# One weight load written as eight strided loads: w_mod in an adaLN decode block

## The chip, the core and the metric

The kernel runs on one core of a Trainium2 chip. A core has five engines with queues of their own: TensorE (PE; its weight loads are listed as PEld), VectorE (DVE), ScalarE (ACT), GpSimd (POOL) and SyncE (SP), which here only issues transfers. Sixteen DMA engines move data between HBM and SBUF, the on-chip memory of 128 partitions. The metric is the device time of one execution in microseconds (us), given as the median of several runs.

## What is computed

One decode step (a batch of two, one token each) of a block with adaptive layer norm: attention over the last 1024 positions of a cached sequence, then a gated feed-forward part. D is 640, there are 32 heads of 192, F is 1536, and everything in HBM is bf16. Cut to what matters:

```python
mod = (silu(c) @ w_mod).reshape(2, 6, 1, 640)     # w_mod: 640 x 3840
sa, ca, ga, sb, cb, gb = mod[:, 0], ..., mod[:, 5]
h = layernorm(x) * (1 + ca) + sa
x = x + ga * attention(h)      # q = h @ wq; K and V: the last 1024 positions of the caches; then @ wo
h = layernorm(x) * (1 + cb) + sb
x = x + gb * ((gelu(h @ w_gate) * (h @ w_up)) @ w_down)
```

## The kernel before

The program first builds a list of operations for each engine and then emits each list in order. An operation names the buffers that it reads and writes; from these names a small scheduler (class `_Sched`, lines 28 to 101) works out which semaphore values it has to wait for. A transfer (`S.dma`) adds 16 to its semaphore when it has landed; `k_dma` (line 239) makes the transfer itself, so that every transfer is listed under line 240. Waits are put ahead of the waiting operation on its own engine's queue (`emit`, line 93), so that everything behind it in that queue waits too.

Loads. Nearly all of them are issued by SP in one fixed order:

1. `ld_wm` (line 294): w_mod, 4,915,200 bytes. Row p of the 128 partitions takes rows 5p to 5p+4 of w_mod, which is 38,400 contiguous bytes of HBM. It lands in the tile r3.
2. `ld_wq` (line 295): the query weights, 128 rows of 61,440 bytes, into the tile r1.
3. The cache loads (line 321), in the order k0, k1, k2, v0, k3, v1 and so on. For each pair of heads and each of K and V there is one slot of a ring of six (`NS`), filled by two transfers, one per batch entry. Each of the two goes to every second partition: 64 rows of 12,288 bytes. The first six slots have no wait. A later one waits until the slot's earlier contents have been used: by the score matmuls (`p_reduce`, line 443) for K, or by `p_pv` (line 488) for V.
4. The output weights wo in four transfers (line 561), the feed-forward weights (lines 565 to 573), with waits on the parts of r1 and r3 that they overwrite.

Four small loads of c and x, four rows of 320 bytes each, are issued by ACT (lines 248 to 251).

Compute ahead of attention. Silu of c (line 332) and a transpose give `scT`. `mod_part(0)` (lines 367 to 385) multiplies it with the first half of w_mod in 20 matmuls, which need all 128 partitions of w_mod, and ACT copies the result to `modC`. `layer_norm("ln1")` follows, then `mod_part(1)`, and two copies (line 389) that lay the normalised row out as the matmul weights `hbm`. The query units (`q_unit`, line 396) multiply `hbm` with slices of wq; the first cannot start before wq has landed.

Attention. A software pipeline over the 16 pairs of heads (lines 526 to 556) multiplies each K slot in place with the query on DVE (`d_mul`, line 431), sums over the head dimension with identity matmuls on PE (`p_reduce`), takes a softmax, and multiplies with the V slot (`p_pv`). PE also runs filler matmuls (line 420).

After attention come the wo matmuls (line 576), the second layer norm, gate and up (`ffn_gu`, line 592), the down projection (line 610), and two small stores of the result (line 625).

Of the kernel before, what the change touches and what calls it, by code (L numbers as in the profile page):

```python
# [103 lines left out]
def bass_adaLN_cond__sliding_block_cached__geglu_ffn__decode_kernel(  # L104
# [15 lines left out]
    P = 128  # L120
    B, _, D = A_x.shape
# [11 lines left out]
    KT = D // P  # L133
# [15 lines left out]
    BIG = -1.0e30  # L149

    NS = 6
    NWO = 4
    GPC = NGG // NWO
    WD_SPLIT = [6, 4, 2]
# [6 lines left out]
    with es:  # L161
        S = _Sched(nc, es)
# [6 lines left out]
        r3 = sb("r3", [P, R3N], BF16)  # L169
# [5 lines left out]
        qbc = sb("qbc", [P, NG, Dh], BF16)  # L175
        ring = sb("ring", [P, NS, J, Dh], BF16)
        ident_b = sb("ident_b", [P, P], BF16)
# [13 lines left out]
        scT = sb("scT", [P, KT, SQ], BF16)  # L191
# [33 lines left out]
        def bank(k):  # L225
            return ("bank", k)
# [3 lines left out]
        sem_wm = S.sem("d_wm")  # L230
        sem_wq = S.sem("d_wq")
        sem_wo = [S.sem("d_wo%d" % i) for i in range(NWO)]
        sem_wg = S.sem("d_wg")
        sem_wu = S.sem("d_wu")
        sem_wd = [S.sem("d_wd%d" % i) for i in range(len(WD_SPLIT))]
        sem_ring = [S.sem("d_ring%d" % i) for i in range(NS)]
        sem_out = [S.sem("d_out%d" % i) for i in range(2)]

        def k_dma(dst, src):
            return lambda e: e.dma_start(dst, src)  # L240
# [9 lines left out]
        for b in range(2):  # L250
# [5 lines left out]
             reads=["ones_f"], writes=["ident_f"], name="ident_f")  # L256
        S.op("pool", lambda e: e.tensor_copy(out=ident_b[:, :], in_=ident_f[:, :]),
             reads=["ident_f"], writes=["ident_b"], name="ident_b")
# [5 lines left out]
             reads=["ones_f"], writes=["par8"], name="par8")  # L264
        S.op("pool", lambda e: e.affine_select(out=noff[:, :], in_=zero_f[:, :], pattern=[[-1, HB]],
                                               compare_op=ALU.is_equal, fill=BIG, base=0, channel_multiplier=1),
             reads=["zero_f"], writes=["noff"], name="noff")
        S.op("pool", lambda e: e.memset(SEL[:, :, :, :], 0.0), writes=["SEL"], name="SEL0")
        S.op("pool", lambda e: e.memset(DS[:, :, :], 1.0), writes=["DS"], name="DS1")
        hb0 = S.op("pool", lambda e: e.memset(hbm_v, 0.0), writes=["hbm"], name="hbm0")  # L270
        S.op("dve", lambda e: e.memset(ps[:, BK_O, 0:ON], 0.0), writes=[bank(BK_O)], name="init_O")
        S.op("dve", lambda e: e.tensor_reduce(out=G32[:, :], in_=ident_f[:, :].rearrange("p (a m) -> p m a", m=SQ), axis=AX.X, op=ALU.add),
             reads=["ident_f"], writes=["G32"], name="G32")
        S.op("dve", lambda e: e.tensor_reduce(out=P4[:, :], in_=ident_f[:, :].rearrange("p (q c) -> p c q", c=HB), axis=AX.X, op=ALU.add),
             reads=["ident_f"], writes=["P4"], name="P4")
        S.op("dve", lambda e: e.tensor_copy(out=Bsel[:, :].rearrange("p (a m) -> p a m", m=SQ),
                                            in_=G32[:, :].unsqueeze(1).broadcast_to([P, NJ, SQ])),
             reads=["G32"], writes=["Bsel"], name="Bsel")

        for z in range(2):  # L280
            for jj in range(2):
# [3 lines left out]
                    reads=["G32"], writes=["SEL"], name="SEL%d%d" % (z, jj))  # L285
            S.op("dve", (lambda z: lambda e: e.memset(DS[:, z, :].rearrange("p (a m) -> p a m", m=SQ)[:, :, 0:2], 0.0))(z),
                 writes=["DS"], name="DS0%d" % z)
# [3 lines left out]
                reads=["P4"], writes=["DS"], name="DS%d" % z)  # L291

        keep = {}
        keep["wm_dma"] = S.dma("sp", k_dma(r3[:, 0:KT * 6 * D], w_mod.rearrange("(p k) n -> p (k n)", k=KT)), sem_wm, writes=["wm"], name="ld_wm")
        keep["wq_dma"] = S.dma("sp", k_dma(r1[:, :], A_wq.rearrange("(p k) n -> p (k n)", k=KT)), sem_wq, writes=["wq"], name="ld_wq")


# [9 lines left out]
        def slot_of(kind, g):  # L307
            return place[(kind, g)] % NS

# [3 lines left out]
        def declare_ring(*consumed):  # L313
            ring_state["done"].update(place[it] for it in consumed)
            while ring_state["next"] < len(items) and (ring_state["next"] < NS or (ring_state["next"] - NS) in ring_state["done"]):
                s = ring_state["next"]
                kind, g = items[s]
                slot = s % NS
                cache = A_v_cache if kind == "v" else A_k_cache
# [45 lines left out]
        mod_pe = []  # L365

        def mod_part(part):
            bk = MB[part]

            def f(e):  # L370
                last = None
                for k in range(KT):
                    for j in range(NJ):
                        last = e.matmul(ps[SQ * j:SQ * j + SQ, bk, 0:3 * DN].rearrange("p (i n) -> p i n", i=3), lhsT=scT[:, k, :],  # L374
                                        rhs=wm_v[:, k, 3 * part * D:3 * (part + 1) * D].rearrange("p (i n) -> p i n", i=3)[:, :, DN * j:DN * j + DN],
                                        start=(k == 0), stop=(k == KT - 1), tile_position=(0, SQ * j))
                return last
            mod_pe.append(S.op("pe", f, reads=["scT", "wm"], writes=[bank(bk)], name="mod%d" % part))
            S.op("act", lambda e: e.activation(out=modC[:, 3 * part:3 * part + 3, :].rearrange("p i n -> p (i n)"),
                                               in_=ps[:, bk, 0:3 * DN], func=ACTF.Copy),  # L380
                 reads=[bank(bk)], writes=[("modC", part)], name="mod%d_evac" % part)
            S.op("dve", lambda e: e.tensor_scalar(out=opc[:, part, :], in0=modC[:, 3 * part + 1, :], scalar1=1.0, scalar2=None, op0=ALU.add),
                 reads=[("modC", part)], writes=[("opc", part)], name="opc%d" % part)

        mod_part(0)
        layer_norm("ln1", 0, 0)
        mod_part(1)
        for h in range(2):
            S.op("dve", (lambda h: lambda e: e.tensor_copy(
                out=hbm_v[:, :, h, :].rearrange("p k (q e b) -> p k q e b", e=2, b=2)[:, :, :, h, :],  # L390
                in_=hT[:, :, 0:2].unsqueeze(2).broadcast_to([P, KT, QP, 2])))(h),
                reads=["hT"], writes=["hbm"], name="hbm%d" % (h + 1))

        qst = {"n": 0, "last": None}
# [164 lines left out]
        r1_dead = [keep["wq_dma"], qst["last"]]  # L559
        for ci in range(NWO):  # L560
            S.dma("sp", k_dma(wo_v[:, ci * GPC * ST:(ci + 1) * GPC * ST, :].rearrange("p (g s) n -> p g (s n)", s=ST),
                              A_wo[ci * GPC * ST * P:(ci + 1) * GPC * ST * P, :].rearrange("(g p s) n -> p g (s n)", p=P, s=ST)),
                  sem_wo[ci], writes=[("wo", ci)], deps=r1_dead, name="ld_wo%d" % ci)
        r3_dead = [keep["wm_dma"], qst["last"], hb0] + mod_pe
        S.dma("sp", k_dma(wg_v.rearrange("p k n -> p (k n)"), B_w_gate.rearrange("(p k) n -> p (k n)", k=KT)), sem_wg,
              writes=["wg"], deps=r3_dead, name="ld_wg")
        S.dma("sp", k_dma(wu_v.rearrange("p k n -> p (k n)"), B_w_up.rearrange("(p k) n -> p (k n)", k=KT)), sem_wu,
              writes=["wu"], deps=r3_dead, name="ld_wu")
# [6 lines left out]

        for ci in range(NWO):
            def f(e, ci=ci):
                last = None
                for t in range(ci * GPC * ST, (ci + 1) * GPC * ST):
                    for j in range(NJ):  # L580
                        last = e.matmul(ps[SQ * j:SQ * j + SQ, BK_M, 0:DN], lhsT=oT[:, t, :], rhs=wo_v[:, t, DN * j:DN * j + DN],  # L581
                                        start=(t == 0), stop=(t == NT - 1), tile_position=(0, SQ * j), skip_group_check=True)
                return last
# [3 lines left out]
             reads=[bank(BK_M), ("modC", 0)], writes=[("lnt", 0)], name="ga_attn")  # L587
        S.op("dve", lambda e: e.tensor_tensor(out=X2[:, 0, :], in0=lnt[:, 0, :], in1=X2[:, 0, :], op=ALU.add),
             reads=[("lnt", 0)], writes=[("X2", 0)], name="x1")
        layer_norm("ln2", 1, 3)  # L590

        def ffn_gu(bk, wv, key):
            def f(e):
# [10 lines left out]
             reads=[bank(BK_Q[0])], writes=["gl"], name="gelu")  # L604
        ffn_gu(BK_Q[1], wu_v, "wu")
        S.op("dve", lambda e: e.tensor_tensor(out=aC[:, :], in0=ps[:, BK_Q[1], 0:FN], in1=gl[:, :], op=ALU.mult),
             reads=[bank(BK_Q[1]), "gl"], writes=["aC"], name="geglu")
        to_contraction(aT[:, :, :], aC[:, :], FT, ["aC"], ["aT"], "aT")
        f0 = 0
        for ci, nf in enumerate(WD_SPLIT):  # L610
            def f(e, f0=f0, nf=nf):
# [10 lines left out]
             reads=[bank(BK_C), ("modC", 1)], writes=["fin"], name="gb_y")  # L622
        S.op("dve", lambda e: e.tensor_tensor(out=orow[:, :], in0=fin[:, :], in1=X2[:, 0, :], op=ALU.add),
             reads=["fin", ("X2", 0)], writes=["orow"], name="outC")
# [55 lines left out]
```

## Time and profile before

| | |
|---|---|
| median of 3 runs | 190.42 us (190.39 to 190.46) |
| the profiled execution | 191.04 us |
| its span, first to last instruction | 189.3 us |
| mean granted TensorE clock | 0.902 |
| HBM read | 76.88 MB |
| PE, DVE, ACT busy | 69%, 48%, 16% of the span |
| w_mod, from issue to landing | 14.5 us |
| wq, from issue to landing | 32.2 us |

The profile is taken from one execution by the hardware profiler. The span leaves out what lies ahead of the first and behind the last instruction of the program, so the execution's own time is 1.74 us longer than its span. Its page has, among other things: busy time in 40 equal slices of the span (4.73 us each), with the share of time in which the sixteen DMA engines were busy and the rate that they moved; the chain of work that ended last; the costliest groups of instructions; and the issues of transfers with the time from issue to landing. The trace behind the page also holds a record of every packet that a DMA engine moved (queue, start, duration, bytes). A row of a transfer, contiguous at both ends, is one packet; each transfer ends on each of its engines with a packet of 4 bytes that writes its semaphore.

### The profile page before, as it was taken

The numbers are of one execution on the slowest core, as the hardware profiler recorded it, in microseconds if no ns is written. First come the engines' busy times: TensorE is split into PE (matmuls) and PEld (weight loads), VectorE is DVE, ScalarE is ACT, GpSimd is POOL, SyncE is SP. The second block draws the span as 40 slices with busy tenths as digits, with TensorE's granted clock in tenths as the row PEclk, the third lists the DMA queues.
The fourth block names the chain that finished last, engine by engine and source line by source line (L and its number), as shares of the span: only waits on it lengthen the run. The fifth ranks groups of instructions, "written<-read, shape, count | busy, mean of one in ns | idle before, by whom it ended". The sixth has DMA issues, their size and how long they took to land.

```text
span 189.3 us, 2631 instructions
## 1 busy us (share of the span) xinstructions
PE 131.5 (69%) x1100; PEld 65.8 (35%) x1100; DVE 91.5 (48%) x140; ACT 29.6 (16%) x75; POOL 3.8 (2%) x15
## 2 busy tenths in 40 slices
PE   0004500989999999997897797898987886333443
PEld 0001200445545435443443343334433454333212
DVE  7101600194855974954956857658559221003421
ACT  1002200122142210210210120120121224000310
POOL 8000000000000000000000000000000000000000
PEclk9999999999999999999999999999999955555555
DMA  7999997999999999999999999999999999999980
GB/s 252 398 507 454 454 415 319 428 418 435 431 415 434 416 430 418 431 419 428 421 436 421 423 423 428 421 421 428 426 428 416 426 417 422 414 433 435 403 328 3
DMA packets 7275, 77.04 MB, mean 407 GB/s; under 512 B 1248, under 2 KB 1248, under 8 KB 2656
## 3 DMA queue, kind: packets, MB, share of 16 engines
q1 hardware_dynamic: 7224, 76.88, 96.5%
q8 instruction: 8, 0.13, 0.3%
q14 instruction: 3, 0.02, 0.0%
q10 hardware_dynamic: 40, 0.01, 0.0%
HBM read 76.88 MB, written 0.00 MB: 406 GB/s over the span
## 4 chain that ended last, share of the span: by engine, by line
DMA 57%; PE 23%; SPq 9%; DVE 8%; issue 1%; ACT 0%; DVEq 0%
DMA ring<-in_A_k_cache_dram 23%; DMA r<-in_A_wq_dram 17%; DMA r<-in_B_w_up_dram 17%; PE ps L446 11%; SPq L240 9%; DVE ring L433 7%; PE ps L406 6%; PE ps L423 1%; PE ps L615 1%; PE ps L597 1%; PE ps L496 1%; PE ps L476 0%; DVE aT L330 0%; PE ps L463 0%; PE ps L477 0%
## 5 line engine op out<-in xcount | busy, mean ns | idle before, releaser
L433 DVE TENSOR_TENSOR ring<-ring,qbc 128x6144 bf16<-128x6144 bf16 x16 | 53.7, 3354 | 33.7 <-DMA ring<-in_A_k_cache_dram 19.9
L446 PE MATMUL ps<-ring,ident_b 128*128 128x512 bf16 x192 | 45.8, 380 | 9.3 <-DVE ring L433 9.3
L446 PEld LDWEIGHTS ps<-ring,ident_b 128*128 128x128 bf16 x192 | 17.9, 98 | 33.0 <-DVE ring L433 14.5
L423 PE MATMUL ps<-qbc,ident_b 128*128 128x512 bf16 x104 | 26.8, 380 | 0.0
L406 PE MATMUL ps<-r 128*128 128x384 bf16 x80 | 15.2, 347 | 11.5 <-DMA r<-in_A_wq_dram 11.5
L503 ACT ACTIVATE On<-ps 128x384 bf16<-128x384 f32 x16 | 7.8, 490 | 46.9 <-PE ps L496 46.9
L374 PE MATMUL ps<-r,scT 128*32 128x480 bf16 x40 | 4.4, 600 | 15.4 <-DMA r<-in_w_mod_dram 15.4
L406 PEld LDWEIGHTS ps<-r 128*128 128x128 bf16 x80 | 8.0, 103 | 18.6 <-issue 14.0
L496 PE MATMUL ps<-ring,E_sb 128*8 128x384 bf16 x256 | 14.3, 348 | 0.1
L581 PE MATMUL ps<-r,oT 128*32 128x160 bf16 x192 | 7.2, 339 | 8.2 <-DMA r<-in_A_wo_dram 8.2
L423 PEld LDWEIGHTS ps<-qbc,ident_b 128*128 128x128 bf16 x104 | 9.2, 107 | 10.4 <-issue 4.3
L468 DVE TENSOR_REDUCE gmn<-ps 1x4 f32<-1x128 f32 x16 | 4.5, 279 | 13.8 <-PE ps L463 13.8
L455 DVE TENSOR_REDUCE S_sb<-ps 128x32 f32<-128x512 f32 x16 | 10.8, 678 | 0.0
L485 ACT ACTIVATE E_sb<-Sb_sb 128x128 bf16<-128x128 f32 x16 | 4.9, 309 | 37.2 <-DVE Sb_sb L482 37.2
L581 PEld LDWEIGHTS ps<-r,oT 128*32 128x32 bf16 x192 | 5.9, 143 | 9.2 <-DMA r<-in_A_wo_dram 9.2
L412 ACT ACTIVATE qbc<-ps 128x384 bf16<-128x384 f32 x8 | 3.9, 490 | 28.9 <-PE ps L406 28.9
L496 PEld LDWEIGHTS ps<-ring,E_sb 128*8 128x8 bf16 x256 | 5.0, 88 | 8.6 <-issue 6.0
L482 DVE TENSOR_TENSOR Sb_sb<-S_sb,ps 128x128 f32<-128x128 f32 x16 | 4.5, 282 | 6.1 <-PE ps L477 6.0
L476 PEld LDWEIGHTS ps<-gmn,ones_f 1*128 1x128 f32 x32 | 4.9, 191 | 6.8 <-issue 6.5
L586 DVE TENSOR_TENSOR lnt<-ps,modC 128x160 f32<-128x160 f32 x1 | 0.3, 325 | 14.2 <-PE ps L581 14.2
L374 PEld LDWEIGHTS ps<-r,scT 128*32 128x32 bf16 x40 | 1.3, 132 | 16.8 <-issue 16.8
L476 PE MATMUL ps<-gmn,ones_f 1*128 1x4 f32 x32 | 6.3, 265 | 0.0
(68 smaller groups left out, 87.6 us busy)
## 6 DMA issues: line engine op xcount, KB each, us to landing
ring<-in_A_k_cache_dram SPq DMA_DIRECT2D x32, 768.0 KB, 14.8
ring<-in_A_v_cache_dram SPq DMA_DIRECT2D x32, 768.0 KB, 15.6
r<-in_A_wq_dram SPq DMA_DIRECT2D x1, 7680.0 KB, 32.2
r<-in_A_wo_dram SPq DMA_DIRECT2D x4, 1920.0 KB, 27.7
r<-in_w_mod_dram SPq DMA_DIRECT2D x1, 4800.0 KB, 14.5
r<-in_B_w_gate_dram SPq DMA_DIRECT2D x1, 1920.0 KB, 33.1
r<-in_B_w_up_dram SPq DMA_DIRECT2D x1, 1920.0 KB, 31.8
r<-in_B_w_down_dram SPq DMA_DIRECT2D x1, 960.0 KB, 31.8
```

What stands on the lines that cost most here:

```text
L240: return lambda e: e.dma_start(dst, src)
L374: last = e.matmul(ps[SQ * j:SQ * j + SQ, bk, 0:3 * DN].rearrange("p (i n) -> p i n", i=3), lhsT=scT[:, k, :], rhs=wm_v[:, k, 3 * part * D: ...
L406: last = e.matmul(ps[:, bk, 0:2 * Dh].rearrange("p (g d) -> p g d", g=2), lhsT=hbm_v[:, k, h, :], rhs=wq_v[:, k, 4 * u * Dh:4 * (u + 1) * ...
L423: last = e.matmul(ps[:, BK_Q[0], 0:512], lhsT=ident_b[:, :], rhs=qbc[:, 0:4, :].rearrange("p g d -> p (g d)")[:, 0:512], start=True, stop= ...
L433: S.op("dve", lambda e: e.tensor_tensor(out=ring[:, ks, :, :], in0=ring[:, ks, :, :], in1=qbc[:, g, :].unsqueeze(1).broadcast_to([P, J, Dh ...
L446: last = e.matmul(o_ap, lhsT=ident_b[:, :], rhs=ring[:, ks, :, ci * GC:(ci + 1) * GC], start=(ci == 0), stop=(ci == NCH - 1))
L455: S.op("dve", lambda e: e.tensor_reduce(out=S_sb[:, z, :], in_=ps[:, z, 0:J * GC].rearrange("p (j c) -> p j c", j=J), axis=AX.X, op=ALU.ad ...
L476: e.matmul(ps[:, BK_T, P:P + HB], lhsT=ones_f[0:1, :], rhs=gmn[:, z, :], start=True, stop=False)
L485: S.op("act", lambda e: e.activation(out=E_sb[:, z, :, :], in_=Sb_sb[:, z, :, :], func=ACTF.Exp, scale=SCALE, accum_out=esum[:, z:z + 1]), ...
L496: last = e.matmul(ps[r:r + 2 * HB, BK_O, 0:ON], lhsT=E_sb[:, z, 2 * jp:2 * jp + 2, :].rearrange("p j c -> p (j c)"), rhs=ring[:, vs, 2 * j ...
L503: S.op("act", lambda e: e.activation(out=On[:, z, :], in_=ps[:, BK_O, 0:ON], func=ACTF.Copy), reads=[bank(BK_O)], writes=[("On", z)], name ...
L581: last = e.matmul(ps[SQ * j:SQ * j + SQ, BK_M, 0:DN], lhsT=oT[:, t, :], rhs=wo_v[:, t, DN * j:DN * j + DN], start=(t == 0), stop=(t == NT ...
```

## The change

The one load of w_mod becomes eight. Load i (i from 0 to 7) takes the rows of partitions i, i+8, i+16, ..., i+120: sixteen rows, eight partitions apart, from and to the same places as before. All eight use the semaphore of the one load, and the matmuls that read w_mod wait for all eight.

```diff
     NS = 6
+    NWM = 8
     NWO = 4
...
-        keep["wm_dma"] = S.dma("sp", k_dma(r3[:, 0:KT * 6 * D], w_mod.rearrange("(p k) n -> p (k n)", k=KT)), sem_wm, writes=["wm"], name="ld_wm")
+
+        keep["wm_dma"] = [S.dma("sp", (lambda i: k_dma(r3[i:P:NWM, 0:KT * 6 * D], w_mod.rearrange("(p k) n -> p (k n)", k=KT)[i:P:NWM, :]))(i),
+                                sem_wm, writes=[("wm", i)], name="ld_wm%d" % i) for i in range(NWM)]
...
-            mod_pe.append(S.op("pe", f, reads=["scT", "wm"], writes=[bank(bk)], name="mod%d" % part))
+            mod_pe.append(S.op("pe", f, reads=["scT"] + [("wm", i) for i in range(NWM)], writes=[bank(bk)], name="mod%d" % part))
...
-        r3_dead = [keep["wm_dma"], qst["last"], hb0] + mod_pe
+        r3_dead = keep["wm_dma"] + [qst["last"], hb0] + mod_pe
```

The bytes, the landing places and all compute stay as they were.

## The prediction

> **What bounds the kernel.** I read the page's slices first, for the resource that is never free.
>
> ```profile
> PE   0004500989999999997897797898987886333443
> DMA  7999997999999999999999999999999999999980
> GB/s 252 398 507 454 454 415 319 428 418 435 431 415 434 416 430 418 431 419 428 421 436 421 423 423 428 421 421 428 426 428 416 426 417 422 414 433 435 403 328 3
> ```
>
> The DMA engines are at nine tenths in all slices but the first, the seventh and the last two, at 415 to 436 GB/s in nearly every one after wq; PE has pauses. (The jagged rates of the first seven slices come from large packets being counted where they start.) Next I asked for the rate in long stretches: the sum of a stretch is more exact than slices.
>
> ```profile
> 1.80:15.40 13.60, 0.00 (x0) 0.00 (x1) 3.93 (x12) 1.62 (x2) 2.71 (x7) 1.00 1.06 434
> ...
> 60.00:150.00 90.00, 81.46 (x576) 37.29 (x574) 58.40 (x74) 13.04 (x43) 0.00 (x0) 1.00 1.01 425
> 152.00:181.00 29.00, 14.95 (x263) 10.20 (x267) 4.92 (x17) 5.06 (x9) 0.00 (x0) 0.51 1.01 421
> ```
>
> The last two columns are the DMA engines' share and GB/s: 434 while w_mod lands, 425 through attention, 421 through the last weights. 76.88 MB at 425 GB/s is 180.9 us of a span of 189.3. So the kernel is one unbroken stream through sixteen DMA engines, with some 2 us ahead of it and a tail behind it. The chain of waits says so with its steps.
>
> ```profile
> 1.26 32.16 DMA r<-in_A_wq_dram
> ...
> 69.86 13.03 DMA ring<-in_A_k_cache_dram
> ...
> 149.07 31.82 DMA r<-in_B_w_up_dram
> 180.89 0.04 issue
> 180.93 1.82 PE ps L597 x20
> ```
>
> The end is released by w_up at 180.89, the next to last weights of the stream, 8.4 us ahead of the end. The PE steps between are where the stream has a backlog of queued slots; they do not stop it, as the DMA share shows. What delays the stream at the front delays everything behind it by as much, since there is no idle DMA time later that could absorb it. w_mod is the very front.
>
> **What the split does to SP's queue.** The issues at the front and their durations:
>
> ```profile
> 0.80 0.39 SPq L240 DMA_DIRECT2D r<-in_w_mod_dram  x1
> 1.26 0.41 SPq L240 DMA_DIRECT2D r<-in_A_wq_dram  x1
> 1.71 3.98 SPq L240 DMA_DIRECT2D ring<-in_A_k_cache_dram  x6
> ...
> 8.32 2.65 SPq L240 DMA_DIRECT2D ring<-in_A_v_cache_dram  x2
> ```
>
> Seven issues are added. From issue to issue it is 0.46 us for the 128-row loads and 3.98/6 = 0.66 us for the 64-row ones; a 16-row one is not in the trace. That bounds the delay of everything behind on SP to 7 x 0.46 = 3.2 up to 7 x 0.66 = 4.6 us. wq is then issued at 4.5 to 5.9 us, and its data is first wanted by the DMA engines when w_mod is through, at 15.3 (0.80 + 14.5). The last of the twelve ring loads ends its issue at 10.97 + 4.6 = 15.6; its turn comes after wq, at 33.4. So I cost the issues at nothing; cover is w_mod's own transfer and then wq's, and without it they would cost 3.2 to 4.6. A DMA engine never runs out either: a row of 38,400 bytes takes 38,400 / (425/16) = 1.44 us (the packet records: median 1.43), and the next load is issued every 0.46 to 0.66.
>
> **What it does per load.** Each load ends with a semaphore packet on each engine: the page's 1248 packets under 512 B are nearly all that (78 transfers x 16, with the small loads of c and x). Seven more of 9 ns and a gap of 6 (packet records) are 0.1 us per engine. Does each load pay a start of its own? The ring answers: 64 loads of 768 KB, about the size of the new ones (600 KB), run back to back at 425. Nothing, then; the upper bound is the start that the first load shows: 14.5 us to land, less 1.0 until the first packet (1.82) and less 8 x 1.44 = 11.5 of moving, leaves 2.0, of which 0.88 is that the sixteen engines' first packets start at 1.82 to 2.70. Seven times 0.88 would be 6.2. [...]
>
> **What it does to the place of the rows.** This is the disputed term. Sixteen engines always move sixteen rows at a time, each at 26.6 to 27.1 GB/s (425/16 and 434/16), whether the rows are of wq, w_mod, a cache or wo. A figure so equal over sources and row lengths is the cap of a path, not of HBM nor of a row's handling. The path has two ends, the DMA engine and the partitions that it writes. All loads at full rate in this trace have rows in every block of four neighbouring partitions: 128 rows, or 64 rows at every second one. The new loads do not. Load i has one row in sixteen blocks of the thirty-two and leaves every second block untouched; loads 0 to 3 use the same sixteen blocks, loads 4 to 7 the others. If the cap belongs to the engine, that is free: 0. If it belongs to a group of neighbouring partitions, half of the groups carry all sixteen rows, two engines share one, and each row takes 2.88 instead of 1.44 us: 8 x 1.44 = 11.5 us more.
>
> Two engines that start d apart lose a little less. The leader is done with loads 0 to 3 early by d and goes to free blocks, which frees d for the other; at the end of loads 4 to 7 this comes once more. Each loses 11.5 - 2d, and with d between 0 and 0.88 that is 9.7 to 11.5.
>
> I take the sharing, with 10.6, the middle. The reasons in the rows: no row shows the cap on the engine's side, since no full-rate load leaves blocks out; and the change can only narrow the spread of the rows. The other bound, 0, stays in the range. [...]
>
> **What else moves.** With w_mod landing at 15.3 + 10.6 = 25.9, mod0 starts then instead of at 15.43. From there it was 8.0 us to the end of the `hbm` copies (23.40), so 33.9, against wq at 33.41 + 10.6 = 44.0: hidden with 10 us to spare, as now. c and x (ACT's queue) take turns with the big rows on the engines: c landed before 11.45, x before 16.60. If each turn doubles, c comes at 1.8 + 2 x 9.6 = 21, x at 1.8 + 2 x 14.8 = 31, from which the first layer norm (18.43 to 23.40, 5 us, and 0.24 for the cast) ends at 36.6: still under 44.0. The wait of the matmuls for eight loads is one wait for the semaphore's last value. The tail behind w_up is as long as now.
>
> Sum: 0 (issues) + 0.1 (semaphores, within the rounding of the next) + 10.6 = 10.6. The profiled execution was 191.04 with its span 189.3; it would be 201.6. The runs' median is 0.62 lower: 190.42 + 10.6 = 201.0. The likeliest case's own range is 199.9 to 202.2 (9.7 and 11.5, with 0.2 for the runs).
>
> **Rivals.**
> 1. *The engine is the cap; nothing happens* (13%): 190.42 + 0.1 = 190.5. For it: the ring's strided loads lose nothing. Against: they touch all blocks.
> 2. *The first bytes come sooner* (14%), the case on the other side. [...]
> 3. *A smaller loss* (11%): a start per load that is partly hidden (up to 6.2), or a shared path on which one engine of a pair goes first, so that its partner is late by four rows, 4 x 1.44 = 5.8, and then both have free blocks. 190.42 + 5.8 = 196.2; 194 to 198.
> Sharing as forecast has 62%.
>
> **How the numbers follow.** A measurement of this kernel tells 0.2% from no change, 190.0 to 190.8. Slower: sharing 62 and the smaller loss 11, 73%. Same: rival 1, 13%. Faster: rival 2, 14%. A range that leaves out rival 2 and the outer edges holds eight in ten: 190.2 to 202.3. It is wide because it spans both bounds of one unknown; the likeliest one's own is 199.9 to 202.2.
>
> **What would show it.** Right: w_mod from first issue to landing at 25 us instead of 14.5, the DMA rate at half (about 215 GB/s) between 2 and 25 us and 425 behind; row packets of 2.9 us; wq landing 10 us later; the end shifted by the same. Rival 1: packets stay at 1.43, wq lands at 33.4, and silu starts before 11.45, since c's packets get an additional turn behind each semaphore packet. [...] Rival 3: some packets at 2.9 and others at 1.43, or gaps between loads. Wrong altogether: w_mod late, but the end not, which would mean idle DMA time that I failed to see.

## The result and the profile after

| | before | changed |
|---|---|---|
| median of 5 runs | 190.42 us (190.35 to 190.48) | 202.89 us (202.79 to 203.10) |
| the profiled execution | 191.04 us | 202.79 us |
| its span | 189.3 us | 201.1 us |

The changed kernel is slower: the ratio is 1.0651, with a 95% interval of 1.0639 to 1.0663. That is 12.5 us, where 10.6 were forecast, and 0.6 us above the upper end of the range. Of the kernels below, the one with four loads of 32 rows had one execution of 276.17 us, in which the matmuls of 512 columns took 0.69 us instead of 0.38 while the rows of w_mod took 1.43 us as in its second profile; it is left out of that kernel's median and ratio.

First the page's slices of the changed kernel; a slice is now 5.03 us.

```profile
PE   0000045009999999999879789879879876433253
...
DMA  7999799969999999999999999999999999999990
GB/s 153 214 245 207 160 391 391 562 293 430 428 416 428 423 421 426 427 425 425 426 425 425 425 418 428 417 431 425 423 430 428 421 415 422 416 419 439 425 375 25
```

The DMA engines count as busy from the start, but in the first five slices, up to 25 us, they move 153 to 245 GB/s; from the tenth to the third from the end it is 415 to 439, about as before. An engine counts as busy in this view for as long as its row takes, however slowly the row moves (a share of 1.05 at 226 GB/s in the first stretch below, where a packet counts whole if it starts there), so the line of GB/s has to be read with the line of shares. Two stretches of the changed kernel (the last column is GB/s):

```profile
1.80:26.00 24.20, 0.00 (x0) 0.00 (x0) 4.17 (x13) 1.62 (x2) 2.72 (x7) 1.00 1.05 226
60.00:150.00 90.00, 81.67 (x571) 39.24 (x578) 61.38 (x75) 15.04 (x46) 0.00 (x0) 1.00 1.01 425
```

226 while w_mod lands, against 434 before, and the same 425 in the attention stage. The chain that ended last, in order of time (start, duration, what):

```profile
0.80 0.64 SPq L241
...
5.93 39.32 DMA r<-in_A_wq_dram
...
161.34 31.32 DMA r<-in_B_w_up_dram
192.66 0.04 issue
192.70 1.82 PE ps L600 x20
```

wq landed at 45.25 instead of 33.41, w_up at 192.66 instead of 180.89: 11.8 us later both, so that what the front of the stream lost reached the end whole. Who waited for whom (us in total, times, longest), in the kernel before:

```profile
PE ps L374 <- DMA r<-in_w_mod_dram: 15.4, 1, 15.4
...
PE ps L406 <- DMA r<-in_A_wq_dram: 11.5, 1, 11.5
```

and in the changed kernel:

```profile
PE ps L377 <- DMA r<-in_w_mod_dram: 27.4, 1, 27.4
...
PE ps L409 <- DMA r<-in_A_wq_dram: 11.4, 1, 11.4
```

The matmuls on w_mod start at 27.4 instead of 15.4. That lateness itself costs nothing, because PE then still waits 11.4 us for wq, as long as before (11.5).

The trace's packet records show the cause at the size of one row. The median row of w_mod, 38,400 bytes, took 2.97 us instead of 1.43. By load, 0 to 7, the medians of the sixteen rows are 2.80, 2.97, 2.98, 2.97, 2.79, 2.96, 2.99, 2.99. In the kernel before, 128 rows on sixteen engines make eight rounds of sixteen rows (the first begins at 1.83 to 2.70 us, the second at 3.91 to 5.00); their medians (of a second profile, below) are 2.09, 1.44, 1.43, 1.44, 1.43, 1.42, 1.42, 1.42.

### The profile page after: what moved, and what is told of

It reads as the page before. It is cut to its first block, busy times and chain, and to the rows that moved or that the text cites. A ratio compares the mean times of both kernels' runs of the same rounds, so it can differ in the third digit from the quotient of the medians.

```text
span 201.1 us, 2629 instructions
## 1 busy us (share of the span) xinstructions
PE 129.9 (65%) x1091; PEld 65.4 (33%) x1100; DVE 91.4 (45%) x140; ACT 29.6 (15%) x75; POOL 3.8 (2%) x15
## 4 chain that ended last, share of the span: by engine, by line
DMA 56%; PE 24%; SPq 11%; DVE 6%; issue 1%; DVEq 0%
DMA ring<-in_A_k_cache_dram 21%; DMA r<-in_A_wq_dram 20%; DMA r<-in_B_w_up_dram 16%; SPq L241 11%; PE ps L449 11%; PE ps L409 8%; DVE ring L436 5%; PE ps L426 1%; PE ps L618 1%; PE ps L600 1%; PE ps L499 1%; PE ps L479 0%; DVE aT L333 0%; PE ps L466 0%; PE ps L480 0%
## 5 line engine op out<-in xcount | busy, mean ns | idle before, releaser
L426 PE MATMUL ps<-qbc,ident_b 128*128 128x512 bf16 x95 | 24.8, 379 | 1.0 <-issue 0.6
L409 PE MATMUL ps<-r 128*128 128x384 bf16 x80 | 16.3, 366 | 11.4 <-DMA r<-in_A_wq_dram 11.4
L377 PE MATMUL ps<-r,scT 128*32 128x480 bf16 x40 | 4.4, 601 | 27.4 <-DMA r<-in_w_mod_dram 27.4
L499 PE MATMUL ps<-ring,E_sb 128*8 128x384 bf16 x256 | 13.4, 331 | 0.2 <-ACT E_sb L488 0.2
L514 PE MATMUL ps<-On,SEL 128*128 128x192 bf16 x32 | 5.6, 258 | 0.8 <-ACT On L506 0.6
```

The source lines that it names most:

```text
L409: last = e.matmul(ps[:, bk, 0:2 * Dh].rearrange("p (g d) -> p g d", g=2), lhsT=hbm_v[:, k, h, :], rhs=wq_v[:, k, 4 * u * Dh:4 * (u + 1) * ...
L426: last = e.matmul(ps[:, BK_Q[0], 0:512], lhsT=ident_b[:, :], rhs=qbc[:, 0:4, :].rearrange("p g d -> p (g d)")[:, 0:512], start=True, stop= ...
L499: last = e.matmul(ps[r:r + 2 * HB, BK_O, 0:ON], lhsT=E_sb[:, z, 2 * jp:2 * jp + 2, :].rearrange("p j c -> p (j c)"), rhs=ring[:, vs, 2 * j ...
L514: e.matmul(ps[:, BK_C, 0:Dh], lhsT=SEL[:, z, jj, :], rhs=On[:, z, jj * Dh:(jj + 1) * Dh], start=(z == 0 and jj == 0), stop=(z == 1 and jj ...
```

## Experiments

The theory, an assumption when the runs began: partitions form groups; the sixteen rows that are under way at a time (in the changed kernel exactly sixteen for 22.2 of the 24.2 us from 1.80 to 26.00, by the packet records) meet two to a group, and share its rate. Rivals were that the rows' places in HBM collide, that a load with a single row for each engine is slow by itself, and that eight loads cost eight starts. All kernels below change only how w_mod is loaded. The row times and ends are from the packet records, those of the four loads of 32 rows from its second profile (below). The edits shown are cut short and are against the changed kernel: `dst <- src` stands for the two sides of the transfer, `wm_src` for w_mod seen as 128 rows, and `...` for what is left out.

| kernel | median row of w_mod, us | last row of w_mod ends | last row of wq ends | median time, us | ratio to before (95%) |
|---|---|---|---|---|---|
| before, again | 1.43 | 14.74 | 32.86 | 190.50 | 1.0001 (0.9992 to 1.0011) |
| changed | 2.97 | 26.45 | 44.82 | 202.89 | 1.0651 (1.0639 to 1.0663) |
| 4 x 32 rows, every 4th | 1.43 | 14.83 | 32.95 | 190.73 | 1.0012 (1.0003 to 1.0022) |
| 8 x 16 neighbours | 5.25 | 44.11 | 63.04 | 221.01 | 1.1596 (1.1577 to 1.1615) |
| source in blocks | 2.95 | 26.26 | 44.60 | 202.60 | 1.0633 (1.0618 to 1.0649) |
| 8 x 128 short rows | 0.185 (4,800 bytes) | 14.84 | 32.97 | 190.95 | 1.0022 (1.0012 to 1.0032) |
| 2 x 64 neighbours | 3.00 | 26.97 | 45.33 | 203.08 | 1.0663 (1.0648 to 1.0679) |
| 8 x 16, every 2nd | 2.99 | 26.78 | 45.23 | 203.26 | 1.0661 (1.0646 to 1.0677) |
| order 0 4 1 5 2 6 3 7 | 2.79 | 25.06 | 43.49 | 201.67 | 1.0590 (1.0574 to 1.0606) |
| two queues | 2.84 | 53.86 | 56.90 | 218.49 | 1.1453 (1.1412 to 1.1495) |

### The ground: the kernel before once more

No edit.

> The kernel before once more, unchanged, for the ground under small differences: ratio 1.000 within 0.002. The profile shown of it lasted 191.04 us, 0.6 above its median, and its first sixteen rows took 1.58 to 2.97 us instead of 1.43. If that slow start is of every execution, the profile here shows it too and lasts about as long as the median; if it belongs to that one execution or to this chip's first rows, the rows here are shorter.

The profiled execution here lasted 190.64 us, next to the median. Its first sixteen rows have a median of 2.09 us, so the slow first rows are in both profiled executions, and the profile shown of before was just 0.4 us longer than this one. Sizes below are against this profile.

### Only the source moved

```diff
-    r3[i:P:NWM, ...]  <-  wm_src[i:P:NWM, :]
+    r3[i:P:NWM, ...]  <-  wm_src[16 * i:16 * i + 16, :]
```

> As the changed kernel on the SBUF side (eight loads, each to every eighth partition), but each load reads sixteen neighbouring rows, one contiguous piece of HBM. The rows of w_mod so go to other partitions, and the modulation is that of permuted weights. Sharing theory: only the place in SBUF counts, packets of 2.97 us and 202.9, within 0.3. HBM distance: back to 190.5.

2.95 us a row and 202.60: as the changed kernel, with every load reading one contiguous piece. The distance of the rows in HBM is not the cause. (The 0.3 us less than in the changed kernel is not clear of the spread: the two intervals overlap.)

### The same count of loads on all partitions

```diff
-    r3[i:P:NWM, 0:KT * 6 * D]  <-  wm_src[i:P:NWM, :]
+    r3[:, 2400 * i:2400 * (i + 1)]  <-  wm_src[:, 2400 * i:2400 * (i + 1)]
```

> w_mod in eight loads again, of the same 600 KB each, but cut along the columns: 128 rows of 4,800 bytes on all partitions. Sharing theory: every group of partitions is used evenly, no loss but what the number of issues and semaphore packets costs, 0.1 to 0.5, so 190.4 to 191. If eight loads instead of one cost by themselves (a start for each, an SP queue that is late), it is towards 203, with gaps between the loads.

190.95, a loss of 0.5. The stretch in which w_mod lands, of this kernel:

```profile
1.80:15.40 13.60, 0.00 (x0) 0.03 (x1) 4.17 (x13) 1.62 (x2) 2.71 (x7) 1.00 1.09 434
```

434 GB/s, the same as before. Eight loads, eight semaphore packets per engine and a wq issued at 5.20 (1.26 before) leave this rate as it was. What there is of a loss fits the short rows: added up for the average engine, the rows of w_mod took 12.5 us here and 12.1 in the profile of before above.

### Which partitions share

Sixteen neighbouring partitions:

```diff
-    r3[i:P:NWM, ...]  <-  wm_src[i:P:NWM, :]
+    r3[16 * i:16 * i + 16, ...]  <-  wm_src[16 * i:16 * i + 16, :]
```

> w_mod in eight loads of 16 neighbouring partitions. Sharing theory, groups of four neighbouring partitions (with those 32 further on): sixteen rows in four groups, four engines to a group, row packets of about 5.9 us, w_mod takes 8 x 5.9 = 47 us instead of 13, the time is about 190.4 + 35 = 225. Sharing by the partition number modulo eight: two rows to each residue, 2.97 us packets, about 203. Few rows per engine: as in the changed kernel, about 203. HBM distance: the source is one contiguous piece of 600 KB, so no loss, about 190.5.

The page's rates for this kernel (slices of 5.48 us):

```profile
GB/s 126 112 112 140 112 112 126 168 392 392 381 410 428 415 426 424 430 427 427 426 413 428 428 419 427 427 427 428 422 419 424 427 420 423 419 419 438 419 394 42
```

Some 112 to 140 GB/s for the first 38 us: about a quarter to a third of the 434 of before. Sixteen rows on sixteen neighbours are much worse than sixteen rows spread by eight, so few rows per engine is not the cause and the partition number modulo eight not the grouping. Four to a group fits, though a row takes 5.25 us and not 5.9, and the time is 221 and not 225.

Thirty-two rows, every fourth partition:

```diff
-    NWM = 8
+    NWM = 4
```

> w_mod in four loads of 32 rows, every fourth partition, so that each load has one row in every block of four neighbouring partitions. Sharing theory (partitions share a path in groups; two of the sixteen rows of the changed kernel fall into each group used, which doubled every row packet to 2.97 us): all groups are used by each load, two rows to a group, two rows to an engine. If one engine gets both rows of a group, packets stay at 1.43 us and the time is 190 to 191; if an engine's two rows lie in neighbouring blocks of four, the engines meet on half of the groups again and it is about 202. Rival, few rows per engine (a load with one row for each engine can't overlap its rows): two rows per engine, so about half of the loss, 196. Rival, HBM (rows 307 KB apart in HBM collide): rows are 154 KB apart now, anything from 190 to 203.

> The four loads of 32 rows at every fourth partition again, for an undisturbed profile: 190.7 us, row packets of 1.43 us throughout, the end of w_mod at 15 us as in the kernel before.

190.73, and in the second run 190.72 with this stretch:

```profile
1.80:15.40 13.60, 0.08 (x4) 0.11 (x8) 4.17 (x13) 1.62 (x2) 2.71 (x7) 1.00 1.05 434
```

The full rate returns, 434 GB/s with rows of 1.43 us. Each load now has a row in every block of four partitions, and by the theory rows of this length mean that those under way at a time do not meet in a group.

Two halves, and sixteen rows within 32 partitions, to see which blocks belong together:

```diff
-    r3[i:P:NWM, ...]  <-  wm_src[i:P:NWM, :]                      # NWM = 8
+    r3[64 * i:64 * i + 64, ...]  <-  wm_src[64 * i:64 * i + 64, :]  # NWM = 2
```

> w_mod in two loads of 64 neighbouring partitions, 0 to 63 and 64 to 127. Which partitions form a group? A block of four with the block 32 further on (or 16 further on): each load reaches eight groups, half of them, four rows of each engine at half rate; packets of 2.97 us, about 202. A block of four with the block 64 further on: each load reaches all sixteen groups, packets of 1.43 us, 190.5.

```diff
-    r3[i:P:NWM, ...]  <-  wm_src[i:P:NWM, :]
+    r3[a:a + 31:2, ...]  <-  wm_src[a:a + 31:2, :]     # a = 32 * (i // 2) + i % 2
```

> Eight loads of sixteen rows at every second partition, each within 32 partitions (0 to 30, 1 to 31, 32 to 62 and so on). Which blocks of four belong together? A block and the one 32 further on: the sixteen rows lie in eight groups, two to a group, packets of 2.97 us, 202.9. A block and the one 16 further on: four groups, four to a group, 5.25 us as with sixteen neighbours, 221.

203.08 with rows of 3.00 us, and 203.26 with rows of 2.99. The first excludes that a block of four shares with the one 64 further on. The second excludes 16 further on. What is left of the three is a block of four with the block 32 further on: by this, sixteen groups of eight partitions. (That a block has four partitions is an assumption; the rows of 5.25 us at sixteen neighbours and of 1.43 at every fourth partition fit it. Steps of 40, 48 or 56 were not among the three, and the row times do not separate them from 32; that such blocks are paired at all, within the same half of the partitions and not within the same 32, is shown by the 3.00 and the 2.99.) The two halves are two large loads of 2.4 MB and lose as much as eight small ones, so the size and the number of the loads have no visible part in it.

The row times of five kernels fit these groups: 1.43 us at every fourth partition, taken as one row to a group; 2.97 in the changed kernel, 3.00 in the two halves and 2.99 at every second partition, taken as two; 5.25 at sixteen neighbours, taken as four.

### Engines that start apart

```diff
-    for i in range(NWM)
+    for i in (0, 4, 1, 5, 2, 6, 3, 7)
```

> The changed kernel's eight loads, issued in the order 0, 4, 1, 5, 2, 6, 3, 7, so that the groups change after each load and not only after the fourth. In the changed kernel the packets of load 4, the first after the change of groups, took 2.79 us and all others 2.97: the leading engine of a pair had free groups for a moment. If that is the gain from engines that start apart, every load but the first has it here: packets of about 2.79, 6 x 0.18 = 1.1 us less, 201.8. If the order is of no account: 202.9.

201.67 was measured, with rows of 2.79 us in every load but the first (2.69). This kernel's stretch, to be held against 226 of the changed kernel:

```profile
1.80:26.00 24.20, 0.00 (x0) 0.00 (x0) 4.17 (x13) 1.62 (x2) 2.71 (x7) 1.00 1.04 244
```

So the same eight loads in another order differ by 1.2 us, and a change of groups is worth about 0.18 us a row (2.97 less 2.79). That this gain is the lead of one engine of a pair over the other, as expected, is not what the packet records show. In the changed kernel all sixteen rows of load 4 took 2.78 to 2.81 us, and those of load 3 still 2.95 to 2.98, though the lead should have shortened the follower's last row of load 3 instead of its first of load 4. And in this kernel, in each of the last three loads, two rows begin 0.02 us apart and 0.38 us ahead of any other, so that neither can lead its partner by 0.18; they took 2.79 like the rest. Where the gain comes from stays open.

### Two queues

```diff
-    S.dma("sp", ..., sem_wm, ...) for i in range(NWM)
+    S.dma("sp" if i < 4 else "act", ..., sem_wm if i < 4 else sem_wm2, ...) for i in range(NWM)
```

> The changed kernel's loads 0 to 3 from SP as before, loads 4 to 7, which use the other half of the groups, from ACT's queue at the same time. If a DMA engine can move rows of both queues at once, all groups work and the loss goes: 190.5 to 192, w_mod through at 15 to 16 us. If it takes the queues in turn, one row at a time, it is the alternate order, 2.79 us a row and 201.7; the rows of loads 4 to 7 then share turns with wq if ACT issues late.

Neither time came out: 218.49, the second worst. The longest wait of PE and the longest piece of the chain, from two views of this kernel:

```profile
PE ps L379 <- DMA r<-in_w_mod_dram: 55.3, 1, 55.3
```

```profile
6.22 48.90 DMA r<-in_w_mod_dram
```

ACT's last load was issued at 6.22 and landed 48.90 us later. ACT's queue holds the loads of c and x first, so its loads of w_mod were issued from 4.19 us on; their first row began only at 11.16 us (packet records), when SP's four loads were nearly through. Why it took 7 us is not shown. What was meant to run beside loads 0 to 3 ran beside wq instead. From then on rows of w_mod and of wq were under way together, and both were slow (wq's rows had a median of 3.7 us instead of 2.27); that they met on the groups fits this and is argued, not shown. The first query unit now waited for what follows from w_mod, not for wq. On what the expectation asked first, the packet records answer: from 11 to 53 us, exactly sixteen large rows of both queues together were under way for 40.6 of the 42 us, and 17 or 18 for 0.8 us (1.1 in the changed kernel, with one queue). With sixteen engines that fits one row at a time for each of them, from either queue; the records used do not name the engine.

## Why the prediction was wrong in its size

**The stream.** Right. DMA was the bound, and the front's delay came out at the end: the last row of the weights ended 12.15 us later than in the second profile of before (196.88 against 184.73), the profiled execution was 12.15 longer.

**The place of the rows.** The mechanism was right: it took the sharing, and the experiments leave no other of the named causes standing. The step that failed is the size of this term, "I take the sharing, with 10.6, the middle": it measured 11.4. Summed by rounds of rows, from the medians above: 0.71 for the first, 6 x 1.55 = 9.3 for those at 2.97, 1.36 for load 4, together 11.4. That half of the groups would carry all sixteen rows, two to a group, at an even division, 2.88 us a row, was the author's assumption: no run ahead of the prediction shows it, and what the runs showed in its place is rows of 2.97 us. Three things were off in the term. First, 0.9 was taken off for engines that start apart (2d, with d the middle of 0 to 0.88). Only 0.18 came off, at load 4, on all sixteen engines alike; at the end of load 7 nothing did, and as said above the records do not bear out the lead as its reason. Second, rows that share take 2.97 us and not 2 x 1.44 = 2.88, so such a row loses 1.55 and not 1.44, which over seven rounds is 0.7 to 0.8 above the bound of 11.5. Third, the first rows are slow in the kernel before anyway (2.09), so the first round loses 0.71 and not 1.44. The second and third nearly cancel, which is luck; what is left is that 0.9 was taken off where 0.18 came off.

**The rest of the 12.15.** It had no term in the prediction. By the last rows (table above) w_mod ended 11.71 later, wq 11.96 and the last weights 12.15. In the 11.71, beside the rows, is a first packet at 2.22 instead of 1.82 us (0.40): the first issue took 0.64 us instead of 0.40, which is 0.24 of it, and the other 0.16 is not explained. With the 11.4 of the rows that makes 11.8, within 0.1 of what was measured. wq lost 0.25 more: the slowest of its first sixteen rows took 3.07 us instead of 2.27. The first of them began beside the last rows of w_mod and may have shared groups with them, but the last of them, begun when w_mod was through, still took 2.50, so that is not all. The remaining 0.19 arises behind wq and is less than two profiles of the kernel before differ by (0.38). The medians of the runs differ by 12.5 and not 12.15, because this second profiled execution of before was 0.2 above the median of 190.42, and that of the changed kernel 0.1 below its own.

**The issues and the loads' own starts.** Costed at nothing and found at nothing that can be told apart: eight full-width loads, with wq issued nearly as late, lost 0.5, and 0.4 of that is in their shorter rows. So the 6.2 that seven further starts were bounded by does not appear either. SP's seven further issues were about 0.59 us each and took wq's issue to 5.93 (forecast 4.5 to 5.9). (The kernel before has 75 transfers with a semaphore packet on all sixteen engines, not 78; nothing rests on it.)

**What else moves.** Right in effect. w_mod was there at 27.4 (forecast 25.9), the `hbm` copies ended at 35.3, wq landed at 45.25: 9.9 us to spare. c and x came sooner than feared (silu at 12.61, the cast of x at 18.42, against 21 and 31). Each row is now followed by a semaphore packet, and in the packet records a small row and its own semaphore packet go in the same gap between two rows of w_mod (0.05 us apart, for instance at 10.93 and 10.98 us), where before 1.4 us lay between them (5.35 and 6.79): it looks as if the small loads had a turn behind that packet too.

**The rivals.** The engine as the cap is excluded by the rows of 2.97 us; the first packet came later (2.22 instead of 1.82 us) and not sooner. A start for each load is excluded by the full-width loads (190.95 us, 434 GB/s while w_mod lands). A pair in which one engine goes first would have shown rows of 1.43 beside rows of 2.9; all rows of the changed kernel took 2.61 to 3.25.

**The range.** Its upper end was the bound of one term plus a little for the spread of runs. It left no room for a shared path to cost more than an even division, nor for the later start.

## What to carry to other kernels

In these runs the rate of a load went by which partitions its rows reach, and not only by how many rows or bytes it has: before a load is cut by partitions, count how many of the sixteen groups found here (a block of four partitions with the block 32 further on) each piece reaches. Thirty-two rows of w_mod at every fourth partition ran at 434 GB/s (1.43 us a row), the 64 cache rows at every second at 425; 16 at every eighth (2.97 us a row) and 64 neighbours (3.00) ran at 226 to 229, about half. Where a load has to be cut, four loads of every fourth row cost 0.3 us here, eight of columns on all partitions 0.5, and eight of every eighth row 12.5.

## What the runs showed that was not expected

By these groups, four rows on one group take 5.25 us, which is 4 x 38,400 bytes / 5.25 us = 29.3 GB/s through the group; two take 2.97, which is 25.9; a single one takes 1.43, 26.9. So two sharing rows lose 4% beyond the division and four gain 9%. No run explains it.

The first issue of a strided load, and of the one of 64 neighbours, took 0.58 to 0.66 us, with the first packet at 2.16 to 2.24. With all partitions or sixteen neighbours it took 0.39 to 0.41, with the first packet at 1.82 or 1.83. No run explains this either.
